# Sink attention then routed attention: longer causal rows cut in even pieces, nine probability buffers, a new instruction order

## The chip, the core and the metric

The kernel runs on one core of a Trainium2 chip. The metric is the device time of one execution in microseconds (us); less is better. The three timed runs of the kernel before are 399.64, 399.67 and 400.88 us, median 399.67. The engines are named as in the profile: PE (TensorE, matrix products; PEld is its weight load), DVE (VectorE), ACT (ScalarE), POOL (GpSimd) and SP, which issues the transfers.

## What is computed

```python
def reference(q, k, v, n_sink, window, w_gate, wq, wk, wv, wo):
    B, H, S, D = q.shape                      # 4, 8, 768, 64; n_sink 4, window 128
    scores = np.matmul(q, k.transpose(0, 1, 3, 2)) / np.sqrt(D)
    keep = is_sink | in_window                # 4 first keys, or the last 128
    a = softmax(np.where(keep, scores, -1e9))
    x = np.matmul(a, v).transpose(0, 2, 1, 3).reshape(B, S, H * D)
    logits = x @ w_gate                       # two of four experts for a token
    for e in range(4):                        # each expert is one causal attention
        q, k, v = x @ wq[e], x @ wk[e], x @ wv[e]
        a = softmax(np.where(causal, -1e9, q @ k.T / 8))
        out += weight(logits, e) * (a @ v @ wo[e])
    return out
```

All is in 32-bit floats.

## The kernel before

The work has two parts for each of four batches. The first attention takes two heads at a time (four pairs in a batch); the second, the experts' causal attention, takes two experts at a time (two pairs in a batch). Queries and keys are cut in six blocks of 128. A **row** is one block of queries of one pair.

A row goes through the engines like this: PE multiplies queries by keys (its scores: `pair.scores`, L812 for the first two batches, L817 otherwise); DVE adds the mask, takes the row minimum of the negated scores and writes to a buffer `p` (L969 for a causal row, L1036 and L1070 in the first attention); ACT takes the exponential in place with its sum (L977, L1041, L1074); DVE inverts the sum (L858, L859); POOL multiplies `p` by it (L984, L1048, L1093); PE transposes `p` in 64x64 pieces (L870); DVE or ACT copies the result to a buffer `pt` (L701, L699); PE multiplies `pt` by the values into `acc` (L843). At the ends stand projections (L1166, L1193) and the output product (L1240).

`wide_rows` makes the six causal rows of a pair of experts: row i has i + 1 blocks of keys. A PSUM bank holds four blocks, so rows of 5 and 6 blocks are cut, in pieces of 4 and 1, and of 4 and 2. Each of the two experts has a `p` buffer of its own, from a ring of eight; rows of the first attention keep both heads in one.

The order is not the order of the code. `Plan.emit` lists all steps engine by engine: for each engine it takes the ready step with the least priority, and a table of some two thousand numbers (`NUDGE`) is added to the priorities. On PE a step also pays for idle time that it would leave (`HURRY`) and for a change of PE's **mode** (`STAY`). PE works in four arrangements of the array: "rows" (scores, L812, L817 and the sinks' product L847), "ROWS" (transposes, L870), "cols" (products with values, L843) and "FULL" (projections and outputs). `STAY` is paid on each change but that between "rows" and "ROWS". Where the planner foresees PE idle in the first 130 us, it puts in products with zeros (L517, `fill`), which keep PE going and compute nothing; below they are called fills.

`kx` is a ring of three buffers with the turned keys of the first two batches. `cmask` is the causal mask: five blocks of zeros and a triangle, set by DVE and POOL at the start.

Of the kernel before, what the change touches and what calls it, by code (L numbers as in the profile page):

```python
# [10 lines left out]
F32 = mybir.dt.float32  # L11
# [26 lines left out]
    "busy_PE": -62.9, " ": -107.1, " busy_PE": -20.9, " busy_PE 0": 25.8, "sink_values_DVE": 1.2, " sink_values_DVE": -48.5,  # L38
    "load_SP": -63.1, " load_SP": 107.7, "again_SP": -2.0, " again_SP": -15.1, "sink_values_ACT": -36.6,
    " sink_values_ACT": -15.3, "sink_values_POOL": 2.3, " sink_values_POOL": -45.4, "sink_values_SP": -5.3,  # L40
    " sink_values_SP": -2.8, "weight_ACT": 99.0, " weight_ACT": 5.0, "weight_POOL": -91.4, " weight_POOL": -43.8,
    "000 ": -53.0, "000 load_SP": 72.1, "tr_PE": -6.1, "000 tr_PE": -67.1, "000 tr_PE 0": -43.5, "fn_DVEACT": 4.7,
    "000 fn_DVEACT": -0.9, "000 tr_PE 1": -38.7, "go_POOL": 17.5, "000 go_POOL": -8.5, "000 tr_PE 2": -27.8,
    "000 tr_PE 3": -1.4, "spread_POOL": 42.9, "000 spread_POOL": 10.3, "differences_POOL": 79.8,
    "000 differences_POOL": -10.7, "band_scores_PE": -1.6, "000 band_scores_PE": -0.1, "000 band_scores_PE 0": -36.0,
    "low_DVE": -2.2, "000 low_DVE": -51.4, "exp_ACT": 21.1, "000 exp_ACT": -15.3, "go_DVE": 14.1, "000 go_DVE": 1.7,
    "norm_POOL": -55.1, "000 norm_POOL": -66.2, "000 tr_PE 4": 24.5, "av_PE": -0.1, "000 av_PE": 4.3, "000 av_PE 0": -26.9,
    "000 band_scores_PE 1": -23.5, "000 tr_PE 5": 57.6, "000 av_PE 1": -26.2, "000 band_scores_PE 2": -22.2,
    "pick_DVE": -1.6, "000 pick_DVE": -31.0, "000 band_scores_PE 3": 10.3, "keep_POOL": -1.4, "000 keep_POOL": -31.6,
    "000 tr_PE 6": 2.8, "tri_DVE": -24.2, "000 tri_DVE": 15.3, "of_sinks_PE": -0.1, "000 of_sinks_PE": -3.1,  # L50
# [239 lines left out]
}  # L290

HURRY = 32.94
# [1052 lines left out]
```

## Time and profile before

| what | value |
|---|---|
| median of three runs | 399.67 us (399.64 to 400.88) |
| the profiled execution's own time | 398.54 us |
| its span, first to last instruction | 396.8 us |
| busy in the span: PE, PEld | 386.5 us (97%), 324.2 us (82%) |
| busy in the span: DVE, ACT, POOL | 313.1, 271.6, 261.9 us |
| granted clock of PE | 0.999 of full speed |

The span is what the rows below count from; the profiled execution took 1.74 us more than its span, and 1.13 us less than the median of the runs. The end of a matrix product is modelled in the profile, so a busy PE says that products follow each other, not that each goes at its best; the start of a product and the start of the next one are the better measure of what it costs.

### The profile page before, as it was taken

The page shows a single profiled execution, that of the slowest core. Times are in us where ns is not written, and L with a number is a line of the kernel's source. Part 1 is how long each engine was busy: PE and PEld are TensorE (multiplying, and loading weights), DVE is VectorE, ACT ScalarE, POOL GpSimd, SP SyncE. Part 2 cuts the span into 40 slices and gives each one's busy share as a digit, 9 for nine tenths or more (in the row PEclk, how much of TensorE's full clock was granted, in tenths as well). Part 3 has the DMA queues.
Part 4 walks back from the last instruction along what each step waited for, and adds up shares of the span by engine and source line. Part 5 has one row for each costly group of instructions (what it writes and reads, how often), then busy time and mean ns, then how long its engine had stood idle before and what let it go on. Part 6 is the DMA issues. An engine that isn't in the chain of part 4 may idle for free.

```text
span 396.8 us, 12884 instructions
## 1 busy us (share of the span) xinstructions
PE 386.5 (97%) x4492; PEld 324.2 (82%) x4492; DVE 313.1 (79%) x1428; ACT 271.6 (68%) x967; POOL 261.9 (66%) x461
## 2 busy tenths in 40 slices
PE   7999999999999999999999999999999999999996
PEld 6767777988888889878887889978888888987874
DVE  5999997796999967969799669699778826569843
ACT  2898896194898867649788768169779825308750
POOL 4779989277679845399919975479956550047840
PEclk9999999999999999999999999999999999999999
DMA  7979997440354105037510332330000000012003
GB/s 166 203 159 162 160 186 137 79 82 3 75 88 82 41 2 81 2 125 158 94 29 2 81 51 33 67 121 28 29 2 2 2 2 2 2 67 94 2 28 132
DMA packets 124032, 28.42 MB, mean 72 GB/s; under 512 B 120576, under 2 KB 120576, under 8 KB 123968
## 3 DMA queue, kind: packets, MB, share of 16 engines
q1 hardware_dynamic: 123968, 27.61, 33.0%
q8 instruction: 35, 0.57, 0.6%
q14 instruction: 29, 0.24, 0.2%
HBM read 21.05 MB, written 6.29 MB: 69 GB/s over the span
## 4 chain that ended last, share of the span: by engine, by line
PE 76%; DVE 13%; POOL 3%; ACT 3%; issue 2%; DMA 1%; POOLq 0%; DVEq 0%; ACTq 0%
PE acc L843 17%; PE b L1166 16%; PE b L817 12%; PE b L870 9%; PE b L1240 9%; PE b L1193 8%; PE b L812 3%; POOL p L984 2%; DVE p L969 2%; DVE b L1067 2%; DVE p L1070 1%; PE acc L847 1%; DVE pt L701 1%; DVE pt L914 1%; ACT p L1074 1%
## 5 line engine op out<-in xcount | busy, mean ns | idle before, releaser
L984 POOL TENSOR_TENSOR p<-p,st 128x128 f32<-128x128 f32 (+5 forms) x96 | 87.5, 935 | 1.8
L699 ACT ACTIVATE pt<-b 128x256 f32<-128x256 f32 (+3 forms) x178 | 64.3, 391 | 16.2 <-PE b L870 14.9
L817 PE MATMUL b<-ks,qs 64*128 64x260 f32 (+4 forms) x672 | 72.4, 326 | 0.0
L977 ACT ACTIVATE p<-p,st 128x128 f32<-128x128 f32 (+5 forms) x96 | 63.6, 665 | 8.2 <-DVE st L969 6.4
L870 PE MATMUL b<-ident,p 64*128 64x64 f32 x1120 | 58.3, 229 | 0.0
L870 PEld LDWEIGHTS b<-ident,p 64*128 64x128 f32 x1120 | 46.5, 138 | 13.4 <-issue 5.7
L817 PEld LDWEIGHTS b<-ks,qs 64*128 64x128 f32 x672 | 53.1, 187 | 5.0 <-DVE st L969 1.0
L1074 ACT ACTIVATE p<-p,st 128x132 f32<-128x132 f32 x128 | 50.8, 405 | 6.8 <-DVE st L1070 4.8
L969 DVE CUSTOM_DVE_ANT_0 p<-b,cmask 128x512 f32<-128x512 f32 (+3 forms) x96 | 50.2, 550 | 2.0 <-PE b L817 1.3
L1048 POOL TENSOR_TENSOR p<-p,st 128x256 f32<-128x256 f32 (+1 forms) x32 | 26.6, 835 | 34.0 <-DVE st L859 9.9
L843 PE MATMUL acc<-pt,v 128*64 128x128 f32 x672 | 46.7, 279 | 0.6 <-DVE pt L701 0.6
L843 PE MATMUL acc<-pt,vn 128*64 128x128 f32 x448 | 42.7, 284 | 1.2 <-ACT pt L699 0.7
L843 PEld LDWEIGHTS acc<-pt,v 128*64 128x64 f32 x672 | 35.9, 136 | 7.4 <-issue 2.4
L701 DVE COPY pt<-b 128x256 f32<-128x256 f32 (+3 forms) x78 | 34.9, 458 | 5.8 <-PE b L870 5.6
L1193 PE MATMUL b<-wvh,x 128*128 128x260 f32 x192 | 36.3, 286 | 0.2 <-DVE st L1036 0.2
L1240 PE MATMUL b<-woh,y 128*128 128x512 f32 x96 | 33.5, 406 | 0.1
L1093 POOL TENSOR_TENSOR p<-p,st 128x512 f32<-128x512 f32 x32 | 33.3, 1042 | 0.0
L1166 PE MATMUL b<-x,wqh 128*128 128x512 f32 (+1 forms) x128 | 33.0, 342 | 0.2 <-DVE ks L752 0.2
L812 PE MATMUL b<-kx,qn 64*128 64x260 f32 (+1 forms) x192 | 30.7, 394 | 2.3 <-DVE kx L701 1.6
L1166 PE MATMUL b<-x,wkh 128*128 128x256 f32 (+1 forms) x128 | 32.4, 341 | 0.0
L1070 DVE CUSTOM_DVE_ANT_0 p<-b,pair_mask 128x132 f32<-128x132 f32 x128 | 32.3, 289 | 0.0
L843 PEld LDWEIGHTS acc<-pt,vn 128*64 128x64 f32 x448 | 24.9, 136 | 8.8 <-issue 2.6
(132 smaller groups left out, 921.0 us busy)
## 6 DMA issues: line engine op xcount, KB each, us to landing
vn<-in_v_dram SPq DMA_DIRECT2D x32, 192.0 KB, 3.3
out_dram<-o SPq DMA_DIRECT2D x24, 256.0 KB, 2.0
qn<-in_q_dram SPq DMA_DIRECT2D x52, 96.0 KB, 2.7
kn<-in_k_dram SPq DMA_DIRECT2D x52, 96.0 KB, 2.6
qn<-in_q_dram SPq DMA_DIRECT2D x6, 192.0 KB, 4.3
kn<-in_k_dram SPq DMA_DIRECT2D x6, 192.0 KB, 4.5
o<-in_moe_wo_dram SPq DMA_DIRECT2D x2, 256.0 KB, 3.6
v<-in_moe_wk_dram SPq DMA_DIRECT2D x4, 128.0 KB, 3.7
```

The source lines that it names most:

```text
L699: nc.scalar.activation(dst(), src(), AF.Copy)
L812: nc.tensor.matmul(o, self.q_of()[hs, qs], self.ks.t[hs, 0, ks], start=True, stop=True)
L817: nc.tensor.matmul(o, self.qs.t[hs, a, qs], self.ks.t[hs, b, ks], start=n == 0, stop=n == 2)
L843: nc.tensor.matmul(o[e * 64:e * 64 + 64], lhs, rhs, start=e not in self.begun, stop=last and self.done == len(self.steps))
L870: nc.tensor.transpose(t[g].t[:, n, :], x[gs], ident[gs, gs])
L969: nc.vector.tensor_tensor_reduce(out=p.t[:, cs], in0=s2[e].t[:, :(c1 - c0) * 128], in1=mask[:, cs], scale=times, scalar=st.t[:, 3, es] if ...
L977: nc.scalar.activation(x, x, AF.Exp, bias=st.t[:, 0, es], scale=-1.0, accum_out=st.t[:, 1, es])
L984: nc.gpsimd.tensor_mul(x, x, st.t[:, 2, e:e + 1].to_broadcast([128, n * 128]))
L1074: nc.scalar.activation(p.t[:, n, :], p.t[:, n, :], AF.Exp, bias=st.t[:, 0, n:n + 1], scale=-1.0, accum_out=st.t[:, 1, n:n + 1])
L1166: nc.tensor.matmul(t.t, w[a][:, c, es], X[b, c].t[:, x, cs], start=c == 0 and m == 0, stop=c == NCH - 1 and m == 2)
L1193: nc.tensor.matmul(t.t[:, :VW], X[b, c].t[:, a, qs], W["wv"][w][:, c, :], start=c == 0 and n == 0, stop=c == NCH - 1 and n == 2)
L1240: nc.tensor.matmul(t.t, Y[b, c].t[:, a, qs], W["wo"][w][:, c, :], start=c == 0 and n == 0, stop=c == EP - 1 and n == 2)
```

## The change

The change has five parts. The numbers of `NUDGE` are all new (two of the first lines are shown), and the order rule of PE has a third constant. Rows of 5 blocks are cut in 3 and 2, rows of 6 in 3 and 3. The `p` ring has nine buffers, and rows of one or two blocks keep both experts in one. The `kx` ring has two buffers. The mask is four blocks wide.

```diff
-    "busy_PE": -62.9, " ": -107.1, " busy_PE": -20.9, " busy_PE 0": 25.8, "sink_values_DVE": 1.2, " sink_values_DVE": -48.5,
+    "busy_PE": 5.2, " ": -68.2, " busy_PE": 82.2, " busy_PE 0": 78.2, "sink_values_DVE": 13.5, " sink_values_DVE": -16.5,
...
-HURRY = 32.94
-STAY = 36.03
+HURRY = 30.10
+STAY = 41.79
+BULK = -8.35
...
+                bulk = {"full": 0.0, "rows": 0.0, "cols": 0.0}
+                if e == PE:
+                    for s in steps:
+                        if s.at[PE] <= free[PE] + 300.0:
+                            bulk[s.mode.lower()] += s.cost[PE]
...
-                    key = (s.prio + (STAY if s.mode.lower() != mode.lower() else 0.0) + HURRY * (t - free[e]) / 100.0, t) if e == PE else (t, s.prio)
+                    key = (s.prio + (STAY - BULK * min(bulk[s.mode.lower()], 2500.0) / 1000.0 if s.mode.lower() != mode.lower() else 0.0) + HURRY * (t - free[e]) / 100.0, t) if e == PE else (t, s.prio)
...
-             "x": (6, 2 * S, F32R), "kx": (3, NB * SW, F32), [...] "p": (8, 768, F32),
+             "x": (6, 2 * S, F32R), "kx": (2, NB * SW, F32), [...] "p": (9, 768, F32),
...
-    cmask = consts.tile([128, S], F32, name="cmask")
+    cmask = consts.tile([128, 512], F32, name="cmask")
...
-            ps, sums = [buf("p", S) for _ in range(2)], []
+            if n <= 2:
+                ps, sums = [buf("p", 2, n * 128)] * 2, []
+            else:
+                ps, sums = [buf("p", n * 128) for _ in range(2)], []
+            one = lambda e, ps=ps, n=n: ps[e].t[:, e, :] if n <= 2 else ps[e].t
+            parts = SPLIT.get(n, [(0, n)])
...
-            for c0 in range(0, n, 4):
-                c1 = min(c0 + 4, n)
+            for c0, c1 in parts:
...
+    SPLIT = {5: [(0, 3), (3, 5)], 6: [(0, 3), (3, 6)]}
```

The instructions stand otherwise on each engine. Three places show how; line numbers of the changed kernel are 8 to 12 higher.

DVE, the first causal row of five blocks, whose two experts write `p_88` and `p_94` before, `p_86` and `p_90` now. Before:

```order
L969 ISA p_88,st_114<-b_122,cmask 128x512
L969 ISA st_114 128x1
L969 ISA p_94,st_114<-b_121,cmask 128x512
L969 ISA st_114 128x1
L969 ISA p_88,st_114<-b_124,cmask,st_114 128x128
L969 ISA st_114 128x1
L969 ISA p_94,st_114<-b_119,cmask,st_114 128x128
```

Now:

```order
L981 ISA p_86,st_114<-b_124,cmask 128x384
L981 ISA st_114 128x1
L981 ISA p_90,st_114<-b_119,cmask 128x384
L981 ISA st_114 128x1
L981 ISA p_86,st_114<-b_120,cmask,st_114 128x256
L981 ISA st_114 128x1
L981 ISA p_90,st_114<-b_121,cmask,st_114 128x256
```

The columns are the same 640 for each expert; the pieces are 384 and 256 where they were 512 and 128.

PE, the output products of the second batch (`woh`, `wol` are the two halves of the weights, `y` the second attention's result). Before, one output tile between scores and transposes:

```order
L817 MATMUL b_121<-ks_74,qs_72 128x128
L817 MATMUL b_120<-ks_74,qs_72 128x128
L1240 MATMUL b_124<-woh,y_0_85 128x512
L1240 MATMUL b_124<-wol,y_0_85 128x512
L1240 MATMUL b_124<-woh,y_0_85 128x512
L1240 MATMUL b_124<-woh,y_0_86 128x512
L1240 MATMUL b_124<-wol,y_0_86 128x512
L1240 MATMUL b_124<-woh,y_0_86 128x512
L870 MATMUL b_123<-ident,p_87 128x64
L870 MATMUL b_119<-ident,p_87 128x64
```

Now, the first of this batch's output tiles, four in a stretch, behind the projection of the values, which is in the same mode:

```order
L1204 MATMUL b_124<-wvh,x_79 128x260
L1204 MATMUL b_124<-wvl,x_79 128x260
L1204 MATMUL b_124<-wvh,x_79 128x260
L1251 MATMUL b_122<-woh,y_0_84 128x512
L1251 MATMUL b_122<-wol,y_0_84 128x512
L1251 MATMUL b_122<-woh,y_0_84 128x512
L1251 MATMUL b_122<-woh,y_0_85 128x512
L1251 MATMUL b_122<-wol,y_0_85 128x512
L1251 MATMUL b_122<-woh,y_0_85 128x512
L1251 MATMUL b_121<-woh,y_0_84 128x512
```

The tile that stood alone, with a change of mode ahead of it and one behind it, stands among others of its mode.

PE, the first scores of the start (`kx_81` and `qn_63` are the first pair's keys and queries). Before:

```order
L517 MATMUL b_123<-nought 64x128 x6
L812 MATMUL b_123<-kx_81,qn_63 128x260
L812 MATMUL b_122<-kx_81,qn_63 128x260
L812 MATMUL b_121<-kx_81,qn_63 128x260
L812 MATMUL b_124<-kx_81,qn_63 128x260
L870 MATMUL b_120<-ident,p_87 128x64
L870 MATMUL b_119<-ident,p_87 128x64
```

Now:

```order
L525 MATMUL acc_125<-nought 64x128 x4
L820 MATMUL b_121<-kx_81,qn_63 128x260
L820 MATMUL b_119<-kx_81,qn_63 128x260
L820 MATMUL b_123<-kx_81,qn_63 128x260
L820 MATMUL b_124<-kx_81,qn_63 128x260
L820 MATMUL b_122<-kx_81,qn_63 128x128
L820 MATMUL b_120<-kx_81,qn_63 128x128
L525 MATMUL acc_125<-nought 64x128 x2
L820 MATMUL b_121<-kx_81,qn_63 128x260
L820 MATMUL b_122<-kx_81,qn_63 128x260
L525 MATMUL b_119<-nought 64x128 x8
```

The scores of the first row, which were the first, stand behind those of four others, and the first transposes of `p` behind two more fills. A row of fills here is twice as many products in the profile, since a product of plain 32-bit floats passes the array in two halves; the same holds for L812 and L843.

## Rows read from the trace of the kernel before

**Rows 1.** The page's first part: busy time, share of the span, instructions.

```profile
PE 386.5 (97%) x4492; PEld 324.2 (82%) x4492; DVE 313.1 (79%) x1428; ACT 271.6 (68%) x967; POOL 261.9 (66%) x461
```

**Rows 2.** Stretches: length, then busy us (instructions) of PE, PEld, DVE, ACT, POOL; PEclk, DMA share, GB/s.

```profile
10.00:20.00 10.00, 9.73 (x128) 7.26 (x125) 9.07 (x56) 8.56 (x40) 7.28 (x15) 1.00 0.96 201
20.00:30.00 10.00, 9.40 (x108) 6.78 (x108) 9.40 (x62) 10.00 (x44) 7.92 (x12) 1.00 0.79 159
30.00:40.00 10.00, 9.88 (x127) 7.31 (x125) 9.60 (x57) 8.54 (x39) 9.77 (x22) 1.00 0.90 160
40.00:340.00 300.00, 297.97 (x3525) 252.92 (x3524) 245.05 (x1105) 217.93 (x779) 207.26 (x352) 1.00 0.30 61
```

**Rows 3.** The waits: who waited for whom, us in total, times, longest.

```profile
PEld acc L843 <- ACT pt L699: 3.9, 9, 0.8
...
PE b L812 <- DVE kx L701: 1.6, 1, 1.6
```

**Rows 4.** PE's timeline from 333 us: start, length, line, tiles, shape, count.

```profile
332.97 1.01 PE L817 MATMUL b<-ks,qs 64*128 64x512 f32 x6
333.91 1.97 PE L843 MATMUL acc<-pt,v 128*64 128x128 f32 x32
335.80 0.96 PE L870 MATMUL b<-ident,p 64*128 64x64 f32 x24
336.57 0.61 PE L817 MATMUL b<-ks,qs 64*128 64x256 f32 x6
337.01 0.66 PE L870 MATMUL b<-ident,p 64*128 64x64 f32 x16
337.47 0.95 PE L817 MATMUL b<-ks,qs 64*128 64x384 f32 x6
338.35 2.40 PE L843 MATMUL acc<-pt,v 128*64 128x128 f32 x40
340.69 0.39 PE L1193 MATMUL b<-wvh,x 128*128 128x260 f32 x1
```

**Rows 5.** PE's timeline: one product with values in steady flow, and scores behind it.

```profile
309.51 0.39 PE L843 MATMUL acc<-pt,vn 128*64 128x128 f32 x4
309.73 0.39 PE L843 MATMUL acc<-pt,dv 128*64 128x128 f32 x4
310.05 0.79 PE L817 MATMUL b<-ks,qs 64*128 64x384 f32 x6
310.68 0.34 PE L870 MATMUL b<-ident,p 64*128 64x64 f32 x5
```

**Rows 6.** PE's timeline: scores of 512 columns, followed by others of their mode.

```profile
100.09 0.95 PE L817 MATMUL b<-ks,qs 64*128 64x512 f32 x6
100.87 0.39 PE L812 MATMUL b<-kx,qn 64*128 64x260 f32 x2
```

**Rows 7.** Groups by shape: scores of L817, busy us, mean ns, idle before.

```profile
L817 PE MATMUL b<-ks,qs 64*128 64x512 f32 x144 | 23.7, 419 | 0.0
...
L817 PE MATMUL b<-ks,qs 64*128 64x128 f32 x144 | 13.2, 274 | 0.0
L817 PE MATMUL b<-ks,qs 64*128 64x256 f32 x96 | 10.6, 306 | 0.0
L817 PE MATMUL b<-ks,qs 64*128 64x384 f32 x48 | 6.7, 365 | 0.0
```

**Rows 8.** PE's timeline at the start: a run of fills and what follows.

```profile
22.14 1.53 PE L517 MATMUL acc<-nought 128*64 128x128 f32 x24
23.60 0.40 PE L870 MATMUL b<-ident,kn 64*128 64x64 f32 x6
```

**Rows 9.** DVE's timeline at the start: the mask and the first keys.

```profile
6.04 0.70 DVE L604 MEMSET cmask<- 128x768 f32 x1
...
8.09 0.34 DVE L701 COPY kx<-b 128x192 f32<-128x192 f32 x1
```

**Rows 10.** PE's timeline at the start: the first scores and what they waited for.

```profile
8.58 0.49 PE L812 MATMUL b<-kx,qn 64*128 64x128 f32 x4 [1.57 <-DVE kx L701]
```

More of the change, by code (lines that the diff above doesn't have):

```diff
@@ L43 @@
[L43 to L47, printed above, removed]
@@ L602 @@
             row_mask[i] = m
-    cmask = consts.tile([128, S], F32, name="cmask")
+    cmask = consts.tile([128, 512], F32, name="cmask")
     nc.vector.memset(cmask, 0.0)
-    nc.gpsimd.affine_select(out=cmask[:, S - 128:], in_=cmask[:, S - 128:], pattern=[[-1, 128]],
+    nc.gpsimd.affine_select(out=cmask[:, 384:], in_=cmask[:, 384:], pattern=[[-1, 128]],
                             compare_op=OP.is_ge, fill=masked, base=0, channel_multiplier=1)
@@ L874, in two, with transposed @@
         return [buf("b", *dims) for _ in range(2)]
-    def transposed(prio, acc, i, ps, cols, block, normed, value, last):
+    def transposed(prio, acc, i, ps, cols, block, normed, value):
         t, n = two(8, 64), 2 * len(cols)
@@ L962, in wide_rows, with low, exp @@
                 mm = plan.step(prio - WIDE_S, {PE: sum(score_cost(w * 128) for _, _, w in runs)}, go,
-                               pair.inputs(i, cols[c0:c1]), s2 + ([] if c0 else [*ps, st]), [pair.qs, pair.ks], fifo="s", mode="rows")
+                               pair.inputs(i, cols[c0:c1]), s2 + ([] if c0 else [*dict.fromkeys(ps), st]), [pair.qs, pair.ks], fifo="s", mode="rows")
                 for e in range(2):
-                    p, es = ps[e], slice(e, e + 1)
-                    def low(e=e, s2=s2, c0=c0, c1=c1, p=p, es=es, n=n, mask=mask, st=st, times=times):
+                    es = slice(e, e + 1)
+                    def low(e=e, s2=s2, c0=c0, c1=c1, one=one, es=es, n=n, mask=mask, st=st, times=times):
                         cs = slice(c0 * 128, c1 * 128)
                         nc.vector.tensor_tensor_reduce(
-                            out=p.t[:, cs], in0=s2[e].t[:, :(c1 - c0) * 128], in1=mask[:, cs], scale=times,
+                            out=one(e)[:, cs], in0=s2[e].t[:, :(c1 - c0) * 128], in1=mask(c0, c1), scale=times,
                             scalar=st.t[:, 3, es] if c0 else BIG, op0=OP.add, op1=OP.min,
                             accum_out=st.t[:, 0 if c1 == n else 3, es])
-                    prev[e] = [plan.step(prio - WIDE_S, {DVE: 78 + 1.04 * 128 * (c1 - c0)}, low, [mm] + prev[e], (), [s2[e], p, st])]
+                    prev[e] = [plan.step(prio - WIDE_S, {DVE: 78 + 1.04 * 128 * (c1 - c0)}, low, [mm] + prev[e], (), [s2[e], ps[e], st])]
             for e in range(2):
-                def exp(p=ps[e], es=slice(e, e + 1), n=n, st=st):
-                    x = p.t[:, :n * 128]
+                def exp(e=e, one=one, es=slice(e, e + 1), st=st):
+                    x = one(e)
                     nc.scalar.activation(x, x, AF.Exp, bias=st.t[:, 0, es], scale=-1.0, accum_out=st.t[:, 1, es])
@@ L981, in wide_rows, with norm @@
             for e in range(2):
-                def norm(e=e, p=ps[e], n=n, st=st):
-                    x = p.t[:, :n * 128]
+                def norm(e=e, one=one, n=n, st=st):
+                    x = one(e)
                     nc.gpsimd.tensor_mul(x, x, st.t[:, 2, e:e + 1].to_broadcast([128, n * 128]))
                 normed.append(plan.step(prio - WIDE_N, {POOL: pool_cost(128 * n)}, norm, [r], (), [ps[e], st]))
-            for c0 in range(0, n, 4):
-                transposed(prio, acc, i, ps, cols[c0:c0 + 4],
-                           lambda e, c, ps=ps, c0=c0: ps[e].t[:, (c0 + c) * 128:(c0 + c) * 128 + 128], normed, value,
-                           c0 + 4 >= n)
+            for c0, c1 in parts:
+                transposed(prio, acc, i, list(dict.fromkeys(ps)), cols[c0:c1],
+                           lambda e, c, one=one, c0=c0: one(e)[:, (c0 + c) * 128:(c0 + c) * 128 + 128], normed, value)
             if i == hi - 1:
@@ L1050, in edge_row @@
         transposed(prio, acc, i, [p], [i - 1 + c for c in range(c0, 2)],
-                   lambda e, c: p.t[:, e, (c0 + c) * SW:(c0 + c) * SW + 128], [nm], value, True)
+                   lambda e, c: p.t[:, e, (c0 + c) * SW:(c0 + c) * SW + 128], [nm], value)
     def both_rows(prio, acc, i, pair, value, diff, vs, made_vs):
@@ L1151, in first @@
         else:
-            wide_rows(prio_of, pair, seen, row_mask, value, None, finish, groups, 0.0 if none_kept else -scale)
+            wide_rows(prio_of, pair, seen, [lambda c0, c1, m=row_mask[i]: m[:, c0 * 128:c1 * 128] for i in range(NB)], value, None, finish, groups, 0.0 if none_kept else -scale)
     def second(b, ep, groups, prio_of, prep_of):
@@ L1175, in second @@
         wide_rows(prio_of, pair, [list(range(i + 1)) for i in range(NB)],
-                  [cmask[:, (NB - 1 - i) * 128:] for i in range(NB)], value,
+                  [lambda c0, c1, i=i: cmask[:, 512 - (c1 - c0) * 128:] if c1 == i + 1 else cmask[:, :(c1 - c0) * 128] for i in range(NB)], value,
                   (lambda i: WT[b].t[:, 2, i, 2 * ep:2 * ep + 2], WT_READY[b]),
```

28 lines of the change are left out of this document (16 added, 12 removed), and 473 rows, old and new, of the table NUDGE.

## The prediction

> **What bounds the kernel now.** I read the page's first part before all else. PE is busy for 386.5 of 396.8 us, DVE for 313.1, ACT and POOL for less [rows 1]. The reader is to see that one engine alone fills the span. An average can hide stages, so the stretches come next. From 40 to 340 us PE is busy for 297.97 of 300 us, while DVE, the next, is busy for 245.05 [rows 2]. PE waits for others there for 2.03 us in all. From 10 to 40 us it looks the same and is not: PE shows 9.73, 9.40 and 9.88 of each 10 us, but part of that is fills, which compute nothing, and ACT is busy for 10.00 of the second of these stretches, DVE for 9.07 to 9.60 [rows 2]. So the start is set by the chain through DVE and ACT, and from 40 us on the time is the length of PE's own stream. The list of waits agrees: the longest sum against PE behind the start is 3.9 us in 9 waits of weight loads for copies to `pt`, and much of that overlaps products under way [rows 3].
>
> What can be gained behind 40 us is therefore what PE's stream itself gets shorter by, plus at most those 2.03 us. For the stream I use the timeline of PE, from the start of a group to the start of the next, since ends are modelled.
>
> **What a change of mode costs.** In steady flow four products with values start 0.22 us after the four before them, 54 ns each; the last four ahead of scores take 0.32 [rows 5], so leaving this mode costs 0.10. In longer groups, 32 products take 1.89 us up to the transposes where 54 ns each would be 1.74, and 40 take 2.34 up to the projection instead of 2.17: 0.15 and 0.17, with some borders between rows inside them [rows 4]. Scores of 512 columns take 0.78 us up to other scores [rows 6] and 0.94 up to products with values [rows 4]: 0.16. Between transposes and scores I see no such price: 24 transposes take 0.77 up to scores, 16 take 0.46, so 32 and 29 ns each [rows 4]; scores of 384 columns take 0.63 up to transposes [rows 5], where 384/512 of 0.78 is 0.59, so 0.04 at most.
>
> Counted through PE's rows of the two programs, the mode changes 346 times before and 308 times now. Of these, 114 and 93 are between "rows" and "ROWS", which I price at nothing; 232 and 215 are the others, **17 fewer**. I take 0.10 each, the value of the one clean group: **-1.7 us**. Its ends: 0.05, if half of that is the border between two rows' work that stays anyway, -0.9; 0.17, -2.9.
>
> Here a rule speaks for much more. The rows say that only some changes cost, about 0.10. The Trainium skill, "TensorE: Matmul & The Clock Gate", section "Single matmul latency", says that a product which cannot hide its drain behind the next one pays a constant of about 166 ns at full clock. If each change of mode made PE drain, an estimate from that page would be 38 x 0.166 = 6.3 us instead of 1.7. The trace disagrees for 114 of the 346 changes, which show 0.04 at most; for the others 0.10 to 0.17 is near it.
>
> **The cut of the longer rows.** There are eight rows of 5 and eight of 6 blocks, six products for a piece. Busy time over count is 165 ns for 512 columns, 92 for 128, 110 for 256 and 140 for 384 [rows 7]. A row of 5 goes from 257 to 250 ns for a pair of products, times 6 times 8: -0.3 us. A row of 6 goes from 275 to 280: +0.2. Together **-0.1 us**. By starts, a row of 6 is 0.78 + 0.44 before and 2 x 0.63 now [rows 4 to 6], +0.3 for eight; at the other end, if only the rows of 5 count and at twice that, -0.6. The columns on DVE, ACT and POOL, and those copied to `pt`, are the same 640 and 768, in as many instructions.
>
> **The fills.** They go from 72 products to 88. A run of 24 takes 1.46 us to the next group, 61 ns each [rows 8], so 16 more are up to 1.0 us. They stand where the planner sees PE idle, and at the start the chain through DVE and ACT sets the pace [rows 2], so I take **0**, with +1.0 as the other end.
>
> **The mask.** Setting `cmask` takes DVE 0.70 us ahead of the first copy of keys, for which PE's first scores wait 1.57 us [rows 9, 10]. Two thirds of the width is 0.23 us less, straight on that path: **-0.2 us**, at worst 0, if what follows on DVE and ACT takes it back.
>
> **The buffers.** A ninth `p`, and one instead of two for short rows, lets DVE write earlier; DVE's waits on POOL, counted in the two programs, go from 125 to 94. What PE can get of this is a part of its 2.03 us of waiting. I take a fifth, **-0.4 us**, as the largest waits are for `pt`, which this does not touch; ends 0 and -2.0. The `kx` ring with two buffers makes a pair's turned keys wait until the pair before the last has its scores; the turns stand on DVE (POOL and PE wait for them), and behind them in its queue stand the mask steps that ACT's exponentials wait for. No row shows that wait. It is 0 if the scores run ahead as they do now, and up to 1.6, the longest wait on `kx` seen [rows 3], if once they do not; I take 0. DMA work is the same in bytes and count.
>
> **The sum**: 1.7 + 0.1 + 0.2 + 0.4 = 2.4 us less, against the profiled execution's 398.54: 396.1. That execution was 1.13 us under the median of the runs, so the forecast on the scale of the median 399.67 is **397.3 us**.
>
> **Rivals.**
>
> *The start gives it back.* The 16 fills cost their 1.0 us, no wait goes, and PE gains half the mode price: 0.9 + 0.1 + 0.2 - 1.0 = 0.2 less, **399.5 us**. For it: the first transposes of `p` now stand behind more scores and two more runs of fills. Against it: ACT and DVE have the same work there.
>
> *The start gets longer than the stream gets shorter.* This one is slower than before. The first row's scores no longer come first; they wait behind four other products, and their exponentials, products with values and `pt` copies with them. If the 1.57 us of wait [rows 10] and the 0.99 us that PE idles from 10 to 40 us [rows 2] come twice, and the fills are paid, that is 3.6 us more, against the 2.4: **400.9 us**. It decides from about 3.6 us on: only if the start lasts that much longer is the kernel measurably slower. For it: ACT has no slack at all from 20 to 30 us [rows 2], so what is late there stays late. Against it: the fills foreseen grow by 1.0 us only.
>
> *The waits go too.* All 2.03 us between 40 and 340 us vanish, in place of a fifth: 2.0 + 2.0 = 4.0 less, **395.7 us**. For it: the loosened `p` ring. Against it: PE's waits are spread thin over many causes, and a new order has new ones.
>
> *Every change of mode costs.* With all 38 at the 0.16 seen for scores of 512 columns [rows 4, 6], 6.1 + 0.7 = 6.8 less, **392.9 us**. This is where the page's rule on the drain would lead. The rows between transposes and scores speak against it.
>
> **How the numbers follow.** A measurement of this kernel can tell about 0.3% from no change, 1.2 us: 398.5 to 400.9. The forecast has 0.46, the waits going 0.10, every change costing 0.06: faster **0.62**. The start giving it back has **0.24**: the same. The longer start, **0.14**: slower. The range runs from 394.0 (397.3 less 1.2 of mode price, 0.5 of the cut and 1.6 of waits) to 400.7, just under the slower case; the two cases left out have 0.20 together. Those that make it faster or leave it within the bound lie inside it but for the last.
>
> **What would show it.** The step of the modes is right if groups of products with values still take 54 ns each plus 0.10 to 0.17 at their ends, and PE's stretch behind the start is shorter by about 1.7 us for the same products. The cut is right if scores of 384 columns still take about 140 ns of busy time each. The fills are free if the first run of products without fills between them starts no later than before; if it starts 1 us later, the second case holds, and 3.6 us later, the slower one. The mask is right if the first scores start near 8.35 us with a wait of about 1.3 us. The forecast is wrong if PE's idle time between 40 and 340 us is over 4 us, or if the DVE copies and exponentials from 10 to 40 us end later than before.

## The result and the profile after

The changed kernel takes **394.42 us** (median, 394.39 to 394.46), the kernel before 399.65 beside it: ratio 0.9862, 95% interval 0.9843 to 0.9881, so 5.2 us less where 2.4 were foretold. A second timing of the same two kernels, in more executions, gave 395.93 against 399.84: ratio 0.9905 (0.9882 to 0.9928), 3.9 us less. Both answers are right, and the experiments show why they differ: executions of both kernels fall into steps of 1 to 1.5 us, which go with PE's granted clock. In the first timing every execution of the changed kernel was on the lowest step; in the second, two of six were. Below, "at full clock" is said of executions whose granted clock is 0.998 or more. There the two kernels stand at 394.46 and 398.54 us (the two profiled executions), 4.1 us apart.

The page's first part for the changed kernel (span 392.8 us, where it was 396.8), to be read beside [rows 1]:

```profile
PE 383.0 (98%) x4508; PEld 325.0 (83%) x4508; DVE 309.9 (79%) x1425; ACT 271.5 (69%) x970; POOL 260.7 (66%) x461
```

PE still fills the span. It is busy for 3.5 us less, with 16 entries more (the fills). The stretches, columns as in [rows 2]:

```profile
10.00:20.00 10.00, 9.69 (x126) 6.97 (x122) 8.79 (x54) 8.79 (x40) 6.09 (x13) 1.00 0.98 219
20.00:30.00 10.00, 9.57 (x114) 7.27 (x112) 9.06 (x60) 10.00 (x47) 7.00 (x11) 1.00 0.76 145
30.00:40.00 10.00, 9.70 (x128) 7.32 (x124) 9.50 (x51) 8.72 (x39) 9.84 (x20) 1.00 0.99 177
40.00:340.00 300.00, 298.82 (x3562) 257.25 (x3562) 246.00 (x1120) 219.83 (x786) 206.86 (x356) 1.00 0.30 60
```

From 40 to 340 us PE waits 1.18 us where it waited 2.03, and gets 37 more products through in the same 300 us (3562 against 3525). ACT fills the stretch from 20 to 30 us as before. The waits named in [rows 3]:

```profile
PEld b L820 <- POOL kx L772: 2.9, 4, 2.0
PE b L820 <- POOL kx L772: 2.2, 2, 1.9
...
PEld acc L851 <- ACT pt L707: 0.8, 2, 0.6
```

For the products with values the 3.9 us of waits for copies to `pt` are down to 0.8. Part of them has moved: over all weight loads, waits for `pt` add up to 5.8 us before and 4.5 now. The first scores now wait for POOL, not for DVE. The start, on DVE's timeline, answers to [rows 9]:

```profile
5.97 0.48 DVE L612 MEMSET cmask<- 128x512 f32 x1
...
7.80 0.34 DVE L709 COPY kx<-b 128x192 f32<-128x192 f32 x1
```

On PE's timeline the first scores, to be read beside [rows 10], and the last product of the program:

```profile
8.46 0.71 PE L820 MATMUL b<-kx,qn 64*128 64x260 f32 x4 [1.90 <-POOL kx L772]
...
388.39 0.40 PE L1251 MATMUL b<-woh,y 128*128 128x512 f32 x1
```

The last product of the kernel before:

```profile
392.50 0.40 PE L1240 MATMUL b<-woh,y 128*128 128x512 f32 x1
```

The keys are copied 0.29 us earlier, the first scores start 0.12 us earlier: their first product is now 260 columns wide, for which POOL adds 20 columns to the keys, 0.40 us behind DVE's copy. From the first scores to the last product the stream is 3.99 us shorter (383.92 to 379.93), and that is where the time went. It went behind 40 us: up to there both kernels have got through the same work, 15.27 us of products each if fills are left out and every product is priced by its start to the next start in steady flow (an estimate from the two traces).

The scores by shape, beside [rows 7]:

```profile
L825 PE MATMUL b<-ks,qs 64*128 64x384 f32 x192 | 24.9, 358 | 0.4 <-DVE st L1081 0.2 <-DVE pt L922 0.2
...
L825 PE MATMUL b<-ks,qs 64*128 64x256 f32 x96 | 10.3, 300 | 0.0
L825 PE MATMUL b<-ks,qs 64*128 64x128 f32 x96 | 9.1, 280 | 0.0
L825 PE MATMUL b<-ks,qs 64*128 64x512 f32 x48 | 7.8, 418 | 0.0
```

Busy time over count is 130 ns for 384 columns, 107, 95 and 163 for the others. What a whole step of six costs is read from starts, on PE's timeline of the changed kernel:

```profile
79.81 0.78 PE L825 MATMUL b<-ks,qs 64*128 64x384 f32 x6
80.42 0.33 PE L855 MATMUL acc<-sk,vs 64*128 64x128 f32 x2
...
126.50 0.58 PE L825 MATMUL b<-ks,qs 64*128 64x128 f32 x6
126.87 0.60 PE L855 MATMUL acc<-sk,vs 64*128 64x128 f32 x4
```

The product behind each is of a row mode too. So six products take 0.61 us with 384 columns and 0.37 with 128; with 512 it is 0.78 and with 256 0.44 [rows 4, 6]. A row of 5 blocks goes from 0.78 + 0.37 to 0.61 + 0.44, 0.10 us less; a row of 6 from 1.22 to 1.22. Eight rows of 5: **0.8 us**, where the prediction had 0.1 for the whole cut.

### The profile page after: what moved, and what is told of

Its sections match the earlier page's. It is cut to its first block, busy times and chain, and to the rows that moved or that the text cites. A ratio compares the mean times of both kernels' runs of the same rounds, so it can differ in the third digit from the quotient of the medians.

```text
span 392.8 us, 12874 instructions
## 1 busy us (share of the span) xinstructions
PE 383.0 (98%) x4508; PEld 325.0 (83%) x4508; DVE 309.9 (79%) x1425; ACT 271.5 (69%) x970; POOL 260.7 (66%) x461
## 4 chain that ended last, share of the span: by engine, by line
PE 81%; DVE 10%; POOL 3%; issue 2%; ACT 2%; DMA 1%; POOLq 0%; DVEq 0%; ACTq 0%
PE acc L851 18%; PE b L1177 18%; PE b L825 13%; PE b L878 10%; PE b L1204 9%; PE b L1251 9%; PE b L820 3%; DVE b L1078 2%; DVE p L1081 1%; PE acc L855 1%; DVE p L981 1%; DMA qn<-in_q_dram 1%; POOL v L680 1%; POOL p L1059 1%; DVE pt L709 1%
## 5 line engine op out<-in xcount | busy, mean ns | idle before, releaser
L989 ACT ACTIVATE p<-p,st 128x384 f32<-128x384 f32 (+5 forms) x96 | 63.6, 669 | 9.4 <-DVE st L981 9.0
L825 PE MATMUL b<-ks,qs 64*128 64x260 f32 (+4 forms) x672 | 69.6, 323 | 0.4 <-DVE st L1081 0.2
L878 PE MATMUL b<-ident,p 64*128 64x64 f32 x1120 | 55.2, 228 | 0.2 <-POOL p L1059 0.2
L878 PEld LDWEIGHTS b<-ident,p 64*128 64x128 f32 x1120 | 44.3, 138 | 11.8 <-issue 6.0
L981 DVE CUSTOM_DVE_ANT_0 p<-b,cmask 128x384 f32<-128x384 f32 (+3 forms) x96 | 45.3, 506 | 1.4 <-ACT o L707 1.1
L1059 POOL TENSOR_TENSOR p<-p,st 128x520 f32<-128x520 f32 (+1 forms) x32 | 26.4, 834 | 14.8 <-DVE st L867 11.3
L1177 PE MATMUL b<-x,wqh 128*128 128x256 f32 (+1 forms) x128 | 33.2, 345 | 0.1
L1177 PE MATMUL b<-x,wkh 128*128 128x512 f32 (+1 forms) x128 | 32.8, 341 | 0.0
L1078 DVE COPY_PREDICATED b<-earlier,b 128x128 f32<-128x128 int32 x128 | 31.4, 288 | 1.2 <-PE b L820 1.1
L1052 ACT ACTIVATE p<-p,st 128x260 f32<-128x260 f32 (+1 forms) x64 | 29.0, 459 | 3.5 <-DVE st L1047 3.4
```

Source lines behind the costliest of these rows:

```text
L825: nc.tensor.matmul(o, self.qs.t[hs, a, qs], self.ks.t[hs, b, ks], start=n == 0, stop=n == 2)
L878: nc.tensor.transpose(t[g].t[:, n, :], x[gs], ident[gs, gs])
L981: nc.vector.tensor_tensor_reduce(out=one(e)[:, cs], in0=s2[e].t[:, :(c1 - c0) * 128], in1=mask(c0, c1), scale=times, scalar=st.t[:, 3, es] ...
L989: nc.scalar.activation(x, x, AF.Exp, bias=st.t[:, 0, es], scale=-1.0, accum_out=st.t[:, 1, es])
L1078: nc.vector.copy_predicated(s2[e].t[:, :128], earlier.bitcast(I32), s2[e].t[:, SW:RW])
L1177: nc.tensor.matmul(t.t, w[a][:, c, es], X[b, c].t[:, x, cs], start=c == 0 and m == 0, stop=c == NCH - 1 and m == 2)
```

## The experiments

All times are medians unless said otherwise; the kernel before ran beside each.

**Run e1: the kernel before once more.** No edit.

> The kernel before, profiled once more. Its profiled execution took 398.54 us, its timed runs 399.6. If the 1.1 us between them is a state of that one execution, this profile shows a span near 397.9 us and a time near 399.6; if the profiler itself makes it 1.1 us shorter, the span is 396.8 again while the timed runs stay at 399.6.

Measured: 399.77 us, ten executions from 398.51 to 400.97. With the granted clock beside them they are 398.51 to 398.59 at 0.999, 399.33 at 0.998, 399.75 to 399.92 at 0.995 to 0.996, 400.74 at 0.994 and 400.97 at 0.991. So the 1.13 us between the profiled execution and the median is no constant: it goes with a loss of clock that most executions have and some have not; e10 below tests that.

**Run e2: more changes of mode, by steps moved.** At 40 places behind 45 us, where PE's steps stood A A B B with a priced change between, they are issued A B A B: 80 changes more.

```diff
+            order.insert(j, order.pop(i))
```

> The changed kernel, all work and buffers as they are; at 40 places behind 45 us two steps of one mode and two of another, A A B B, are put A B A B. That makes 80 more changes of mode that are priced (215 to 295) and nothing else. If a change costs 0.145 us, as the gaps at the changes in the two traces say, it takes 11.6 us more (406.0 us); at the 0.10 of the forecast 8.0 more (402.4); if the gain came from fewer waits and a change is nearly free because PE waits anyhow, under 3 more (below 397.4).

Measured: 410.34 us, 15.9 more than the changed kernel's first timing, 0.20 for a change. PE's idle time from 40 to 340 us went from 1.18 to 3.46 us, so waits came with the moves, and by the time alone the price is not told apart from them. At the 0.15 us a change that e17 gives below, 80 changes are 12 us of the 15.9.

**Runs e3 and e4: fewer changes, by steps moved.** In the kernel before (e3) and in the changed one (e4), 14 and 13 PE steps are moved forward to the last step of their own mode, wherever what they read should be there by then: 28 and 26 changes fewer.

```diff
+            order.insert(found[1], order.pop(found[0]))
```

> The kernel before, with its eight p buffers, its cut and its own table; in its finished order 14 steps of PE are moved forward to a step of their own mode, where their inputs and slots are free by the planner's times. Changes that are priced fall from 232 to 204. If changes alone make the gain at 0.145 us each, 4.1 us less than the kernel before (395.5 us); at 0.10, 2.8 less (396.9); if the ninth buffer and the shorter waits were what mattered, 0 to 1 less, or more time, since steps behind the moved ones come later.

> The changed kernel with the same treatment: 13 steps moved, priced changes from 215 to 189. At 0.145 us each 3.8 us less than the changed kernel (390.6 us), which would beat both; at 0.10, 2.6 less (391.8). If the changed kernel's order leaves no slack, the steps that now come later make PE wait and it gains under 1 us or loses.

Measured: 405.23 and 399.71 us. At full clock e3 took 403.73 (one execution) and e4 399.63 to 399.79, both 5.2 to 5.3 us **slower** than their originals there. PE's idle time from 40 to 340 us, from the stretches of e3 and then of e4:

```profile
40.00:340.00 300.00, 295.37 (x3431) 250.92 (x3430) 241.89 (x1089) 213.75 (x766) 207.07 (x352) 1.00 0.30 61
```

```profile
40.00:340.00 300.00, 296.88 (x3510) 255.48 (x3509) 242.18 (x1101) 216.90 (x773) 207.35 (x356) 1.00 0.30 60
```

It is 4.63 us (2.03 before) and 3.12 (1.18). A change of mode that is taken out alone costs more than it gives. Idle time shows only 2.6 and 1.9 us of the loss; the rest must be waits too short to show as idle behind products whose ends are modelled, which is argued, not shown. What the new order does is to have fewer changes at no more waiting.

**Runs e5 and e14: the cut by itself, from both sides.** e5 is the changed kernel with rows cut 4 and 1, 4 and 2 again, in the order of steps made for the new cut; e14 the kernel before with the new cut, in its old order. The steps are planned as for c0 to c1, and the blocks from r0 to r1 computed. In e5 the mask of four blocks puts its triangle on the fourth block of a first piece too, which changes the output and no instruction.

```diff
+            for (c0, c1), (r0, r1) in zip(parts, REAL.get(n, parts)):
+    REAL = {5: [(0, 4), (4, 5)], 6: [(0, 4), (4, 6)]}
```

> The changed kernel with its order of steps kept as it is, but rows of 5 and 6 blocks cut into pieces of 4 and 1 or 4 and 2 again. Counted through the products of the two traces, each at its steady start-to-start time, the new cut makes the stream 0.9 us shorter. If that is so, this run is 0.9 us longer than the changed kernel: about 395.3 us. The forecast's term for the cut was 0.1 us (0.3 less for rows of 5, 0.2 more for rows of 6): 394.5 us. A rival: with pieces of 4 in places made for pieces of 3, copies and exponentials are late and PE waits: 396 us or more, with PE's idle time between 40 and 340 us well over the 1.18 us of the changed kernel.

> The kernel before with its order of steps on every engine kept, and rows of 5 and 6 blocks cut into pieces of 3 and 2 or 3 and 3. By the products' steady start-to-start times the cut makes the stream 0.9 us shorter: 397.7 us where the kernel before shows 398.6 at full clock, or 398.9 against 399.8 in the median. By the forecast's term it gives 0.1. If pieces of 3 in places made for 4 make PE wait, as the undone cut did in the new order (3.2 us), it is slower: 400 to 402.

Measured: e5 398.58 us, 4.1 more than the changed kernel at full clock; e14 401.55, and 400.12 in its only execution at full clock, 1.6 more than the kernel before there. Both expectations of 0.9 fell, and the rival with the waits held. The shorter products are in the trace (the steady starts above), but pieces that arrive at other times than the order was made for make PE wait. Of e5's 4.1 us, PE's idle time shows 0.56 (1.74 us from 40 to 340 us, where it was 1.18) and the cut accounts for 0.8; that the rest is shorter waits is argued. The cut and the order belong together, so these two runs do not give the cut's worth by themselves.

**Run e6: no fills.** All 88 fill entries of the changed kernel left out, which compute nothing.

```diff
+        order = [x for x in order if x[2].cost]
```

> The changed kernel without any of its 88 fill products, all other steps in the same order. The forecast held that fills cost nothing, as they stand where PE waits: no difference, 394.4 us within 0.3. The case of the start giving it back had 16 fills cost 1.0 us, so all 88 up to 5: 389 to 393 us. A third theory: the executions of the kernel before fall into steps of about 1.2 us that go with a granted clock of 0.991 to 1.0, the changed kernel shows 0.999 to 1.0 in all, and fills keep PE from going quiet at the start. Then this run has a granted clock under 0.998, and is 1 to 4 us longer, 395.5 to 398.5 us, with executions scattered by steps.

Measured: 398.26 us, scattered from 397.27 to 399.55, with a granted clock of 0.973 to 0.987. The stretches of its profile:

```profile
8.00:20.00 12.00, 9.50 (x78) 7.53 (x80) 7.85 (x48) 7.76 (x35) 5.60 (x14) 0.65 1.11 222
20.00:30.00 10.00, 9.86 (x82) 6.86 (x80) 8.44 (x47) 7.72 (x31) 5.02 (x8) 0.74 0.69 127
30.00:40.00 10.00, 8.45 (x79) 6.73 (x77) 7.89 (x53) 8.94 (x43) 9.31 (x16) 0.83 0.66 115
```

The third theory holds: PE's clock is granted at 0.65 to 0.83 on average of these stretches, where it was 1.00 with fills. Leaving the fills out costs 3.8 us, nearly all of it in the start: at 40 us e6 has got through 11.9 us of products, by the same estimate as above, where the two kernels have 15.3.

**Run e7: more changes between the row modes.** At 13 places, scores and transposes that stood A A B B stand A B A B; the edit is that of e2.

> The changed kernel with 13 places behind 45 us where two steps of scores and two of transposes that stood as A A B B are issued as A B A B: 26 more changes between the two row modes, which the forecast prices at nothing, and as many of the other changes as before. If such a change costs 0 to 0.04 us, 394.4 to 395.5 us. If it costs the 0.148 us of the others, 3.8 more, 398.3 us. Waits that come with the moved steps would show as idle time of PE between 40 and 340 us over the 1.18 us of the changed kernel.

Measured: 398.82 us (398.77 to 398.85 at full clock), 4.4 more. By the time alone the 0.148 would hold. The trace says otherwise. PE's timeline at one of the places:

```profile
292.46 0.34 PE L911 MATMUL b<-ident,p 64*128 64x64 f32 x4
292.61 0.60 PE L858 MATMUL b<-ks,qs 64*128 64x260 f32 x6
293.05 0.22 PE L911 MATMUL b<-ident,psk 64*128 64x64 f32 x2
293.10 0.41 PE L911 MATMUL b<-ident,p 64*128 64x64 f32 x8
293.32 0.56 PE L858 MATMUL b<-ks,qs 64*128 64x128 f32 x6
```

Six scores of 260 columns take 0.44 us up to the transposes, as much as six of 256 up to transposes in [rows 4]; ten transposes take 0.27 up to scores. Next to nothing is paid there; over all such borders of e7, scores up to transposes show nothing at the middle one and transposes up to scores 0.03 us, so 26 of them are under 0.8 us of the 4.4. PE's idle time from 40 to 340 us is 3.03 us instead of 1.18, and the waits of weight loads for `pt` grew with it: the moved steps wait. About 2 us stay that no row shows as idle. So "every change of mode costs" falls for the row modes, by the trace and not by the time.

**Run e8: the ninth buffer in the old order.** The kernel before, every engine's order kept, with a ninth `p` of 544 columns, the `p` buffers given out in the order of first writing, and the mask of 512 columns (which again changes the output and no instruction).

```diff
-"p": (8, 768, F32)
+"p": (9, 768, F32)
```

> The kernel before with its order of steps on every engine kept, a ninth probability buffer (of 544 columns, which is all that the memory leaves) in the ring, and the causal mask of 512 columns. If the loosened ring itself gives PE back what it waited for, as the forecast's term had it, 0.4 to 2.0 us less than the kernel before, and 0.2 for the mask: 397.5 to 399.2 against 399.7 us. If the buffer only gives the planner room for another order, nothing in this order: 399.7 us, or 399.5 with the mask. If the narrower mask or the ring changes how the start meets the clock, the executions no longer fall into the steps of 398.5, 399.7 and 400.9 us.

Measured: 398.15 us, and 398.03 to 398.18 in the six executions at a clock of 0.999 or more: 0.4 to 0.5 less than the kernel before on that step, of which 0.29 is the earlier start of the first scores (8.29 us). The buffer in the old order is worth some 0.2 us at most. Its profiled execution fell on a high step (400.46 us), and shows where the clock goes. The stretches:

```profile
7.00:8.00 1.00, 0.00 (x0) 0.00 (x0) 1.00 (x3) 0.00 (x0) 0.00 (x0) 1.00 1.16 260
8.00:9.00 1.00, 0.71 (x9) 0.74 (x11) 0.14 (x1) 0.00 (x0) 0.20 (x1) 0.68 1.20 230
9.00:10.00 1.00, 1.00 (x11) 0.97 (x10) 0.78 (x5) 0.58 (x3) 0.00 (x0) 0.50 1.34 228
10.00:11.00 1.00, 1.00 (x7) 0.81 (x6) 0.58 (x3) 0.61 (x5) 0.00 (x0) 0.50 1.36 218
11.00:12.00 1.00, 1.00 (x16) 0.88 (x14) 1.00 (x7) 1.00 (x5) 0.00 (x0) 0.61 0.89 138
12.00:13.00 1.00, 1.00 (x16) 0.78 (x14) 0.66 (x6) 1.00 (x6) 0.48 (x1) 1.00 0.96 285
```

PE was idle from 6.3 to 8.3 us, waiting for the first keys. Then it computes, and the clock is granted at half (1.2 GHz in place of 2.4) for about 3 us. The Trainium skill ("TensorE: Matmul & The Clock Gate", "HAM oscillation — how this bites in real kernels") describes such a chain, a wait for data and behind it products at half clock; this trace agrees, with 0.50 behind the wait, but other executions of the same kernel lose nothing there.

**Runs e9 to e13: the clock at the start.** e9 is the changed kernel again. e10, e11, e12 and e13 put fills directly ahead of the first scores: 16 products in the kernel before (e10), 20 in the changed one (e11), 20 with each `p` given out in the order of first writing (e12), 12 in the changed one (e13).

```diff
+        first = next(n for n, (_, _, s) in enumerate(order) if s.eng == PE and s.mode == "rows")
+        order.insert(first, (0.0, 0, Step(0.0, {}, lambda: self.fill("cols", ("acc", 1), 6), (), (), (), 0, "cols", ())))
```

> The changed kernel once more, in more executions and beside the kernel before on the same chip. The loss of clock at the start was seen in one execution in ten of kernels with this start. If that holds here too, the median is 394.4 us, with one or two executions in ten at 395.6 to 396. If the changed kernel never loses clock there, all lie between 394.3 and 394.6. A third theory: part of the gain came from the shorter warm-up run of products seen in its profile (3.89 us where others show 4.64): then the median is 395.1.

> The kernel before with 16 more fill products directly ahead of the first scores, where PE waits 1.57 us for their keys, and nothing else changed. If the steps of its executions (398.5, 399.7, 400.9 us) come from PE being idle there, upon which the clock is granted at half for some microseconds, the executions now all lie near 398.5 us, the median 1.1 to 1.3 us lower than 399.8. If the clock falls for another reason, the steps stay and the median is 399.7 to 400.0. If the fills delay the scores, up to 0.9 us more: 399.4 to 400.7.

> The changed kernel with 20 more fill products directly ahead of the first scores, where PE waits up to 1.90 us. If only the clock is protected, 394.4 us in every execution and a granted clock of 0.998 or more. If the fills run into the time of the first scores, up to 1.1 us more: 394.5 to 395.5 us.

> As the run with more fills in the changed kernel, and each of the nine probability buffers is given out in the order in which it is first written by VectorE, not in the order of the scores on TensorE; every engine's order is the same. If waits for a free probability buffer still hold VectorE back somewhere, 0.2 to 0.6 us less than the run with fills alone: 393.8 to 394.2 us. If nothing waits for these buffers any more, no difference: 394.4 us.

> The changed kernel with 12 more fill products directly ahead of the first scores (24 entries of the trace, some 1.3 us, where the run with 20 more had 2.4 us and its scores 0.4 us late). If the steps between 394.5 and 396 us are the clock that is lost after PE's idle time there, nearly all executions now lie at 394.4 to 394.7 us, with a granted clock of 0.998 or more, and the median is over 1 us under that of the changed kernel on this chip (395.9 us). If the steps stay as they were, 395.5 to 396.

Measured: e9 395.93 us; two executions at 394.46 and 394.49 with a clock of 1.0, four at 395.93 to 396.17 with 0.995 or 0.996. The changed kernel loses clock too, more often than expected, and the shorter first run of products changes nothing (the third theory there falls: e13, with 4.30 us there, has 394.42 in its profiled execution). e10 398.75 us against 399.84 for the kernel before beside it; eight of twelve executions lie between 398.65 and 398.76, the others at 398.88, 399.25, 399.68 and 400.0; those of 399.68 and 400.0 had a clock of 0.999 or more, so something else delayed them, for which these runs give no cause. e11 395.42, e12 395.20: the clock stays, but 40 entries of fills take 2.40 us and the first scores are late (8.88 us in e11). e12's executions lie inside the range of e11's, so the ring makes no difference that these runs can tell. e13, with 24 entries:

```profile
6.79 1.53 PE L527 MATMUL acc<-nought 128*64 128x128 f32 x24
8.46 0.71 PE L822 MATMUL b<-kx,qn 64*128 64x260 f32 x4
```

The scores start at 8.46 us, as without these fills. All six executions lie between 394.42 and 394.70 us; median **394.46 us**, ratio to the kernel before 0.9874 (0.9849 to 0.9899). Over e10 to e13 all 26 executions had a clock of 0.998 or more, where four of six of e9 and eleven of seventeen of the kernel before, on the chip of e9 to e12, had less. This version beats the kernel before, and the changed one wherever that loses clock; in the same series e15, which has the changed kernel's start, lost some in one execution of four.

**Run e15: the mask.** 256 columns of the mask are set a second time.

```diff
+    nc.vector.memset(cmask[:, :256], 0.0)
```

> The changed kernel with 256 columns of its causal mask set once more on VectorE at the start, so that the mask takes about as long as it did. The forecast had the narrower mask give 0.2 us: 0.2 us more here, 394.7 us at full clock, with the first scores 0.2 us later than 8.46. If the scores now wait for another engine's copy of keys (the trace names GpSimd's), nothing: 394.4 to 394.5 at full clock.

Measured: 394.90 to 394.94 us at full clock, 0.45 more than the changed kernel. DVE's timeline has 0.39 us more ahead of the keys' copy (8.19 against 7.80), PE's first scores start at 8.84 instead of 8.46: the time on DVE goes straight through to the end. The mask's term was right in kind.

**Runs e16 to e18: the price of a change by itself.** The same 36 fills (144 entries) are put into the changed kernel behind 45 us, and no step is moved: between products with values (e16, no change more), between steps of the row modes (e17, 72 changes more), between steps of the full mode (e18, 72 more).

```diff
+            if not (a.cost and b.cost and a.mode.lower() == b.mode.lower() == "rows" and 45000.0 < a.begun < 340000.0):
+                continue
...
+            order.insert(m, (0.0, 0, Step(0.0, {}, lambda w=where: self.fill("cols", w, 1), (), (), (), 0, "cols", ())))
```

> The changed kernel with 36 pairs of fill products (four entries of the trace each) put behind 45 us between two steps of products with values, which are in the same mode: no change of mode more. In steady flow four such entries take 0.22 us: 36 x 0.22 = 7.9 us more, 402.4 us at full clock.

> The changed kernel with the same 36 fills put behind 45 us between two steps of the row modes (scores or transposes): 72 changes of mode more than with the fills between products with values. At the forecast's 0.10 a change, 7.2 us over that run: 409.6 us. At 0.148, which the trace gives where a product's start to the next start is set against the mean product, 10.7 over: 413.0. At half of the forecast's price (part of it being a border of two steps that is there anyway), 3.6 over: 406.

> The changed kernel with the same 36 fills put behind 45 us between two steps of projections or output products: again 72 changes more than with the fills between products with values. If a change costs alike from any mode, as far over that run as the fills among the row modes: 7.2 us at 0.10, 10.7 at 0.148. If leaving the full mode is cheaper, as the 0.09 us at the end of output products in the trace suggests, 6.5 us.

Measured at full clock: e16 400.32 to 400.51 us, e17 408.33 to 408.59, e18 414.33 to 414.5. e16 is 5.9 over the changed kernel where 7.9 were expected, so 2 us of its fills fell into waits. e17 is 8.1 over e16, 0.11 us for a change; e18 is 14.0 over, 0.19. Both figures are net of waits that take some of the added time back. PE's timeline of e16, then of e17, then of e18:

```profile
51.94 0.39 PE L545 MATMUL acc<-nought 128*64 128x128 f32 x4
52.16 0.61 PE L871 MATMUL acc<-pt,vn 128*64 128x128 f32 x8
```

```profile
95.68 0.77 PE L845 MATMUL b<-ks,qs 64*128 64x384 f32 x6
96.39 0.44 PE L545 MATMUL acc<-nought 128*64 128x128 f32 x4
96.75 0.62 PE L845 MATMUL b<-ks,qs 64*128 64x256 f32 x6
```

```profile
55.32 0.40 PE L1197 MATMUL b<-x,wql 128*128 128x512 f32 x1
55.64 0.44 PE L545 MATMUL acc<-nought 128*64 128x128 f32 x4
56.01 0.73 PE L1197 MATMUL b<-x,wqh 128*128 128x512 f32 x2
56.58 0.39 PE L1197 MATMUL b<-x,wql 128*128 128x512 f32 x1
56.81 0.63 PE L1197 MATMUL b<-x,wqh 128*128 128x512 f32 x2
57.28 0.39 PE L1197 MATMUL b<-x,wql 128*128 128x512 f32 x1
```

A fill among its like takes 0.22 us. In e17 the scores take 0.71 up to the fill instead of 0.61, and the fill 0.36 instead of 0.22. In e18 the product ahead of the fill takes 0.32 instead of 0.23, the fill 0.37, and the two products behind it 0.57, where two such take 0.47 in flow (56.81 to 57.28). So a change has a price on both sides: about 0.10 us ahead of the first product of the new mode, and 0.05 to 0.10 behind it. A whole group of products with values, from the changed kernel, shows the same:

```profile
125.08 0.44 PE L851 MATMUL acc<-pt,vn 128*64 128x128 f32 x4
125.35 0.39 PE L851 MATMUL acc<-pt,dv 128*64 128x128 f32 x4
125.56 0.39 PE L851 MATMUL acc<-pt,vn 128*64 128x128 f32 x4
125.78 0.39 PE L851 MATMUL acc<-pt,dv 128*64 128x128 f32 x4
126.10 0.59 PE L878 MATMUL b<-ident,p 64*128 64x64 f32 x12
```

The first four products take 0.27 us, the next fours 0.21 and 0.22, and the last four 0.32.

To have all of it, the traces are set against that of the changed kernel product by product, from the sixth product ahead of each place to the sixth behind it. At the middle one of its 36 places e16 takes 0.22 us more, e17 0.51 and e18 0.56. Less the fill's own 0.22 that is **0.15 us for a change** between products with values and the row modes, and **0.17** between them and the full mode. On average over the places e17 has 0.48, so 0.13 a change, since some of its places took up a wait. Between the places the three streams get back 2.1, 3.5 and 0.3 us in waits, which is why the times give 0.11 and 0.19: the 14.0 us of e18 are 72 changes at 0.17 and the 1.8 us that e16 got back and e18 did not.

## Why the prediction was right and wrong

**Direction and mechanism: right; the sizes were not.** PE's own stream was the time, and it got shorter behind the start, but 2.4 us were foretold and 5.2 measured, 4.1 at full clock. The parts behind 40 us are: 23 changes of mode at 0.15, about 3.5 us; the cut, 0.8; four entries of fills at 45 us, 0.2 the other way. That makes 4.1, where the stream is 4.0 shorter there. The waits give nothing on the whole: PE's idle time behind 40 us is 1.0 us less, and waits too short to show as idle take about as much back. This last is an estimate, from what the groups of products take beyond their steady prices and the price of their changes (10.0 us in both kernels, idle time included). The parts are each read on their own; that they fit the total is a check, not a proof, since e5 and e14 show that cut, order and waits do not come apart.

**What a change of mode costs: the largest term that failed.** It had 1.7 us, for 17 changes at 0.10; it is about 3.5, for 23 at 0.15. The 0.10 came from [rows 5], which begin inside a group of products with values and so show the end of a group and not its beginning. The longer groups of [rows 4] had the whole price, 0.15 and 0.17, and I put the difference down to borders between rows. The count of 17 is that of the whole program (232 to 215). Behind 40 us it is 23 (208 to 185); the new start has six more, around fills and where PE waits anyway. The rule of 166 ns from the Trainium skill ("TensorE: Matmul & The Clock Gate", "Single matmul latency") is near what stood at the priced changes, 0.15 (e17) and 0.17 (e18), and far from what stands between the row modes, 0.03 at most (e7); it fails for "each change", not for these.

**The cut of the longer rows: too small.** It had 0.1 us, with 0.6 as the far end, and gives 0.8. It was worked out from busy time over count, in spite of my own remark that the ends are modelled. By starts six products with 128 columns take 0.37 us, not the 0.55 that 92 ns each make, so a row of 5 gained 0.10 us and not 0.04, and a row of 6 lost nothing. The starts were there in the trace of before, and I used them for the rows of 6 alone.

**The sum's last step failed too.** I added 1.13 us because the profiled execution was that much under the median, as if every execution carried it. It goes with a loss of clock at the start, which an execution has or has not. The first timing had none of it, and the median fell by those 1.1 us besides the 4.1 of the stream; that no execution there lost clock was luck, as e9 shows, where most did and the forecast's 397.3 stands against 395.9. I had the granted clock of 0.999 in the profile and only the times of the other runs, and read no cause into their gap.

**Fills: right.** Twelve of the 16 entries more stand ahead of 40 us, and at 40 us both kernels have got through the same work. What I did not see is what fills buy: without them the clock falls (e6).

**Mask and buffers.** The mask was to give 0.2; e15 shows that DVE's time there passes through, and the new order takes part of it back by a wider first product that waits for POOL, so the scores start 0.12 earlier, at 8.46 us where 8.35 was foretold; by 40 us that is no longer seen. The buffers were to give a fifth of 2.03 us. PE's idle time from 40 to 340 us fell by 0.85, but with the shorter waits counted in, nothing is left of it. e8 gives the buffer alone some 0.2 at most in the old order. The `kx` ring shows one wait of PE behind the start, 0.28 us at 49 us (before there was one of 0.33 at 25 us), so nothing, as taken.

**Rivals.** "The start gives it back" and "the start gets longer" did not happen: the first scores came earlier, and at 40 us the same work is done. "The waits go too" was near by its number (395.7), by another way: less than half of the idle time is gone, and the changes of mode give what it gave to the waits. "Every change of mode costs" had the right price (0.16) for the changes that cost, and put it on those between the row modes too, which do not.

## What to carry to other kernels

Price products by start to next start over a whole step, from the trace of before: busy time over count showed 0.1 us of the cut's 0.8. Read a change of mode over a whole group, since part of its price stands behind the group's first product. Where PE waits at the start, look at each execution's granted clock before trusting the median, and fill the wait to its end and no further: too few fills can lose clock (e9), too many delay the work (e11). Changes of mode are worth taking out only with an order in which nothing then waits: 26 taken out by hand cost 5.3 us.

## What was not expected of the hardware

After some 2 us of idling at the start PE's clock was granted at half for about 3 us in some executions of a kernel and in others of the same kernel not at all (e8: six of ten at 0.999 or more, three at 0.994 to 0.996). The length of the idling does not tell which: the changed kernel's two profiles idled for 1.90 and 1.96 us (e9) and kept the clock at 1.00, e15's for 1.52 us and lost it, 0.50 from 10 to 12 us. In e14's profile it was 0.51 from 9 to 15 us:

```profile
8.00:9.00 1.00, 0.45 (x4) 0.48 (x6) 0.41 (x2) 0.00 (x0) 0.20 (x1) 0.53 1.27 244
9.00:15.00 6.00, 6.00 (x44) 4.83 (x44) 3.50 (x22) 3.50 (x15) 2.15 (x3) 0.51 1.18 221
15.00:16.00 1.00, 1.00 (x10) 0.65 (x6) 1.00 (x9) 0.76 (x5) 0.84 (x2) 1.00 0.77 153
```

That execution took 402.63 us against 400.12 at full clock: 2.5 us for 6 us at half speed, which alone would be 3 us, so work that waits for others seems to hide part of it. And a change between the two row modes is all but free (0.03 us at most), while one between products with values and the row modes costs 0.15 and the full mode 0.17. The trace gives scores and transposes the same form, 64*128, and products with values 128*64 and projections 128*128: the price stands where that form changes.
